# One chain of scales for the later projection weights, sums of magnitudes pinned to their place, and TensorE in program order through the opening

## The chip, the cores and the metric

The kernel runs on one core of a Trainium2 chip. The metric is the device time of one execution in microseconds (us). The engines are TensorE (PE in the profile, PEld for its weight loads), VectorE (DVE), ScalarE (ACT), GpSimd (POOL) and SyncE (SP), which issues the DMAs.

## The reference

A transformer block with parallel branches, on a sequence of 2048 rows of width 512, all in float32:

```
xn  = layernorm(x)                                    # no gain, no bias
q, k, v = xn @ wqkv                                   # 32 heads of 16
att = softmax(q k^T / 4) v                            # every row sees every row
mlp = gelu(xn @ w1 + b1) @ w2 + b2                    # 512 -> 1792 -> 512
out = x + att @ wo + mlp
```

## The kernel before, in words

**Numbers.** Matrices are multiplied as pairs of 16-bit halves: a high part and the rest, so each product of float32 operands is three matmuls. Before a weight is split into its halves it is divided by a power of two, taken from its largest magnitude (for some weights from an average of magnitudes). `scales` (L122) makes such factors: each column of a 128 x n tile holds one value per partition, TensorE transposes it (L125), VectorE takes the maximum of each row (L127), TensorE spreads the n results over all partitions (L130), and VectorE keeps the exponent bits (L137) and takes reciprocals (L139). `split_pool` (L147) then writes the halves, one instruction on ScalarE and two on GpSimd.

**Heads and units.** The query and key weights are worked off in four column blocks m = 0 to 3 of 128 columns (8 heads each). Scores are computed for groups of four heads. A *unit* is 128 queries by 512 keys of one group of four heads: `s_half` (L247) issues, for each head, four matmuls 62 x 32 (tile `pS`), and VectorE takes the row maximum of each head's scores (tile `mt`, L259), 0.6 us each. Two neighbouring heads lie on the two halves of the partitions. Scores use three PSUM banks in rotation. The maxima go through DRAM (`m_d`) into two extra rows of the queries' operand, and 19 units later (`LEAD`) the scores are computed again, transposed, with the maximum subtracted, and ScalarE takes the exponential (L304, tile `pe`). The value products (`pV`) follow. Into the gaps go matmuls of a filler: the rest of the value projection, the projections of m = 1 to 3, then the MLP and the output projection.

**The opening** is the program up to the first exponential. It loads and normalizes x in four blocks of 512 rows (`stats`, `transpose_x`), projects q and k of m = 0 for each block (`project`), stores them to `qk_d` and reads them back stacked (`stacks`, L403), computes the value projection of nine row tiles (`v_tiles`), and runs the first sixteen units, four after the projection of each block (`tile_and_unit`, L846: two heads' scores, three matmuls of the value projection, and the same again). Beside this it loads the weights w1, w2 and wo in 16 pieces of 512 KB (`chunk`, L719, three buffers, issued by SyncE), and ScalarE sums the magnitudes of each piece (`measure`, L830, instruction L835). `fetch` keeps one piece ahead. Each step of the generator `ms` is one piece; `MEASURE` says how many steps follow each unit of a block (its first entry belongs to the last four units).

**Order.** In the opening the order of each engine's instructions is chosen by a scheduler, which may move an instruction ahead of the program when it takes its operands to be ready. From unit 16 on all five engines keep the order of the program (L1022); there, `later` and `by_slots` hand out small pieces of work unit by unit.

**The later weights.** `prep_qk` (L458) takes the largest magnitudes of a pair of weight blocks (tile `wq` -> `am_qk`, L461), calls `scales` for two columns and splits. For m = 1 it is called in the opening (L927), for m = 2 and 3 in the slots, when the projection of the block before begins (L952). `prepare` (L970) makes the ten scales of w1, b1, w2 and wo in the first slots and then splits these weights.

Of the kernel before, what the change touches and what calls it, by code (L numbers as in the profile page):

```python
# [9 lines left out]
F32 = mybir.dt.float32  # L10
# [20 lines left out]
VW = DH + 1  # L31
LEAD = 19
FAST, MEAN, SLOW = (4, 4), (3, 4), (3, 3)
MEASURE = (2, 0, 1, 1)
HALF = 1300
POOL_NS = 2500
TAIL = 5
# [14 lines left out]
def layer_kernel(ctx: ExitStack, tc: tile.TileContext, x, wqkv, wo, w1, b1, w2, b2, out):  # L52
# [144 lines left out]
            product(user, dst[j:j + 32], lhs[:, j:j + 32], rhs, start=start, stop=stop)  # L197


    scale_of = {}  # L200

    def fetch_scale(m):

# [247 lines left out]
    def load_qk(m):  # L451
        wf = []
        for w in range(2):
            wf.append(ph.tile([P, D], F32, name="wq", bufs=2).rearrange("p (c n) -> p c n", n=P))
            nc.sync.dma_start(wf[w], wqkv[:, w * D + m * P:w * D + (m + 1) * P].rearrange("(c p) n -> p c n", p=P))
        return wf

    def prep_qk(m, wf, bank, ready_w):  # L458
        am = work.tile([P, 2], F32, name="am_qk", bufs=2)
# [248 lines left out]
    with ExitStack() as st1:  # L708
# [6 lines left out]
        def load_x(t):  # L715
            xs[t] = px.tile([P, D], F32, name="xs", bufs=8)
            nc.sync.dma_start(xs[t], x[t * P:(t + 1) * P, :])

        def chunk(src):  # L719
            wf = ph.tile([P, 4 * W], F32, name="wch", bufs=3)  # L720
            v = wf.rearrange("p (a b) -> p a b", b=src.shape[2])
            if len(loads) < 17:
                nc.sync.dma_start(v, src)
            else:
                later(2, lambda: nc.sync.dma_start(v, src), True)
            return v
# [9 lines left out]
        wov = wo.rearrange("(c p) n -> p c n", p=P)  # L736
        every = [w1v[:, :, i * W:(i + 1) * W] for i in range(7)]
        every = every + [w2v[:, 2 * i:2 * i + 2, :] for i in range(7)] + [wov[:, 0:2, :], wov[:, 2:4, :]]
        every = every + every
        amx = work.tile([P, 16], F32, name="amx")  # L740
        am_all = work.tile([P, 10], F32, name="am_all")
        fac1 = []

        def fetch(k):
            while len(loads) <= min(k + 1, 31):
                loads.append(chunk(every[len(loads)]))
            return loads[k]

        for t in range(4):
            load_x(t)  # L750
        wfs = [load_qk(0)]
        for t in range(4, 8):
            load_x(t)
        wvv = wqkv[:, 2 * D:3 * D].rearrange("(c p) n -> p c n", p=P)
# [41 lines left out]
        def transpose_x(sb, c):  # L796
            cs = slice(sb * QB, (sb + 1) * QB)
            pt = vbank()
            for i in range(4):
                nc.tensor.transpose(pt[:, i * P:(i + 1) * P], xs[4 * sb + i][:, c * P:(c + 1) * P], ident)  # L800
            nc.scalar.activation(xt[:, 0, c, cs], pt, AF.Copy)  # L801
            if sb and c % 2:
                pf = ph.tile([P, QB], F32, name="pf", bufs=2)
                nc.scalar.activation(pf, pt, AF.Copy)
                nc.gpsimd.tensor_tensor(xt[:, 1, c, cs], pf, xt[:, 0, c, cs], op=ALU.subtract)
            else:
                nc.vector.tensor_tensor(xt[:, 1, c, cs], pt, xt[:, 0, c, cs], op=ALU.subtract)
            if c == NC - 1:
                for t in range(4 * sb + 8, min(4 * sb + 12, NT)):
                    load_x(t)  # L810
# [19 lines left out]
        def measure():  # L830

            for n in range(16):
                v = fetch(n)
                dst = am_all[:, n:n + 1] if n < 7 else amx[:, n:n + 1]
                nc.scalar.activation(v, v, AF.Abs, scale=1.0 / SPREAD, accum_out=dst)  # L835
                yield

        ms = measure()
# [55 lines left out]
            run(whole(project(0, w, 0, ready_w[0], lambda: (vbank(), None), True)))  # L894
        for w in (1, 0):
            stacks(0, w, [0])
        free[:] = ["T", "D", "T", "V", "T"]
        for c in range(NC):
            transpose_x(1, c)
        some(pv, 2)  # L900
        for sb in range(1, NQB):
            ln = stats(sb + 1) if sb < 3 else iter(())
            for w in (1, 0):
                pj = whole(project(0, w, sb, ready_w[0], lambda: (vbank(), None)))
                for n in range(3):
                    some(pj, 4)
                    some(pv, 1)
                    if sb == 2:
                        some(ln, 3)
                run(pj)  # L910
            run(pv)
            for w in (1, 0):
                stacks(0, w, [sb])
            wfs.append(load_qk(sb))
            if sb == 1:
                clear(1)
            for j in range(4):
                tile_and_unit(4 * sb - 4 + j)
                some(ms, MEASURE[sb])
                if sb == 1:  # L920
                    some(ln, 4)
                elif sb == 2:
                    transpose_x(3, j)
            if sb == 1:
                for c in range(NC):
                    transpose_x(2, c)
        pq = prep_qk(1, wfs[1], sbank, ready_w)  # L927
        for j in range(4):
            some(pq, 2)
            tile_and_unit(NT - 4 + j)  # L930
            some(ms, MEASURE[0])
        run(pq)
        run(vs)
        nc.sync.dma_start(b1_s, b1.rearrange("(f p) -> p f", p=P))
        pos[0] = 16

# [3 lines left out]
        def rest():  # L940
            for k in range(8):
                later(8 + 4 * k, lambda k=k: stacks(1, 1 - k // 4, [k % 4]), True)
            for k in range(4 * NQB):
                c, cols = k % 4, slice(k // 4 * QB, k // 4 * QB + QB)
                later(10 + 3 * k, lambda c=c, cols=cols: nc.sync.dma_start(xn_d[:, :, c, cols], xt[:, :, c, cols]), True)
            for t in range(NV, NT):
                yield v_group(t, wvh, dbank)
            for m in range(1, 4):
                while m not in ready_w:
                    yield None  # L950
                if m < 3:
                    by_slots(prep_qk(m + 1, wfs[m + 1], sbank, ready_w))  # L952
                for sb in range(NQB):
                    for w in (1, 0):
                        yield project(m, w, sb, ready_w[m], dbank)
                    if m == 3 and sb == 2:
                        for n in range(2):
                            fetch_w1(n)
                        fetch_x(0)
# [8 lines left out]
                   (0, then))  # L968

        def prepare():  # L970
            yield from ms
            am = am_all
            nc.vector.tensor_reduce(am[:, 7:8], b1_s, axis=AX.X, op=ALU.max, apply_absolute_value=True)
            nc.vector.tensor_reduce(am[:, 8:9], amx[:, 7:14], axis=AX.X, op=ALU.max)
            nc.vector.tensor_reduce(am[:, 9:10], amx[:, 14:16], axis=AX.X, op=ALU.max)
            box = []
            yield
            yield from scales(am, 10, sbank, box)
            inv, fac = box
            fac1.append(fac)  # L980

            nc.vector.reduce_max(gs[:, 0:1], fac[:, 0:8], axis=AX.X)
            nc.gpsimd.tensor_tensor(gs[:, 3:4], fac_v[0][:, 0:1], fac[:, 9:10], op=ALU.mult)
            yield
            nc.vector.reciprocal(gs[:, 1:2], gs[:, 0:1])
            nc.gpsimd.tensor_tensor(gs[:, 2:3], gs[:, 0:1], fac[:, 8:9], op=ALU.mult)
            yield
            nc.vector.tensor_scalar_mul(gs[:, 1:2], gs[:, 1:2], 0.5)
            ended = [True]
            for n in range(16):  # L990
                v = fetch(16 + n)
                while not ended[0] or len(v_done) < NT:
                    yield
                ended[0] = False

                def then(wh=None, n=n):
                    ended[0] = True
                    later(2, lambda: put(wh, n), True)

                def put(wh, n):  # L1000
                    for a in range(2):
                        if n < 7:
                            later(a, lambda a=a: nc.sync.dma_start(w1_d[n, :, a], wh[:, a]), True)
                        elif n < 14:
                            later(a, lambda a=a: nc.sync.dma_start(w2_d[:, :, 2 * n - 14 + a], wh[:, :, a]), True)

                if n >= 14:
                    i = 2 * (n - 14)
                    split_steps(wo_s[:, 0, i:i + 2, :], wo_s[:, 1, i:i + 2, :], v, inv[:, 9:10], then)
                    continue  # L1010
                if n < 7:

                    wh = ph.tile([P, 2, 2, NC, P], F16, name="wsp", bufs=3)
                    split_steps(wh[:, :, 0], wh[:, :, 1], v.rearrange("p c (a n) -> p a c n", n=P), inv[:, n:n + 1],
                                lambda wh=wh, then=then: then(wh))
                else:
                    wh = ph.tile([P, 2, 2, D], F16, name="wsp", bufs=3)
                    split_steps(wh[:, 0], wh[:, 1], v, inv[:, 8:9], lambda wh=wh, then=then: then(wh))
            while not ended[0]:
                yield  # L1020
# [234 lines left out]
```

## Time and profile before

| | |
|---|---|
| median of 3 runs | 1506.36 us (1505.23 to 1510.21) |
| the profiled execution | 1509.12 us, span 1507.3 us |
| granted TensorE clock, mean | 0.996 |
| TensorE busy | 1484.6 us |
| VectorE busy | 1387.1 us |
| ScalarE busy | 1257.4 us |
| GpSimd busy | 661.4 us |
| first exponential | 108.5 us |
| bytes moved | 123.75 MB, mean 82 GB/s |

Times within a profile are counted from the start of the span. In a timeline row stand the start, the time from the first instruction's start to the last one's end, the engine, the line, the operation, the tiles written and read, their shapes and the number of merged instructions; in brackets the engine's idle time ahead of it and what ended that. In the chain of waits each row is the stretch by which a piece of work moved the end. SPq is SyncE issuing DMAs.

### The profile page before, as it was taken

Reading aid. Unit: us, or ns where it says so; the run is one execution under the profiler, and the core shown is the slowest. Engines: PE = TensorE matmul, PEld = TensorE weight load, DVE = VectorE, ACT = ScalarE, POOL = GpSimd, SP = SyncE. Lnnn points to the kernel's source line nnn. Section 1 sums busy time; section 2 is a strip of 40 time slices with the busy share of each in tenths; the row PEclk is TensorE's granted clock in tenths of the full one; section 3 lists DMA queues with packets and bytes.
Section 4 is the critical chain, followed back from the end, with each engine's and each line's share of the span. In section 5 each row is a group of like instructions: output and inputs, shape, how many; then the busy total and the mean of one; then the engine's idle time right before and its main releaser. Section 6 shows DMA issues by size and latency. Waiting matters only on the chain.

```text
span 1507.3 us, 87890 instructions
## 1 busy us (share of the span) xinstructions
PE 1484.6 (98%) x39995; PEld 815.2 (54%) x39995; DVE 1387.1 (92%) x2333; ACT 1257.4 (83%) x2348; POOL 661.4 (44%) x686
## 2 busy tenths in 40 slices
PE   8999999999999999999999999999999999999998
PEld 3335555555555555555555555555555555555554
DVE  8789889999899999999999999999999999999933
ACT  4738878888899888899988889998888998888884
POOL 4112778423777311377821147862115786121210
PEclk9999999999999999999999999999999999999998
DMA  8730867224222310131111111121112210211432
GB/s 248 242 95 7 247 200 238 72 73 125 85 76 73 99 29 27 42 85 43 43 57 43 51 50 39 44 78 57 37 27 61 70 36 19 57 54 33 137 92 93
DMA packets 113357, 123.75 MB, mean 82 GB/s; under 512 B 24668, under 2 KB 84956, under 8 KB 112984
## 3 DMA queue, kind: packets, MB, share of 16 engines
q1 hardware_dynamic: 112984, 118.14, 26.4%
q8 instruction: 312, 5.11, 1.4%
q14 instruction: 61, 0.50, 0.1%
HBM read 80.61 MB, written 37.34 MB: 78 GB/s over the span
## 4 chain that ended last, share of the span: by engine, by line
PE 87%; DVE 8%; issue 1%; DMA 1%; ACT 1%; POOL 0%; SPq 0%; ACTq 0%; POOLq 0%
PE pV L168 25%; PE pD L168 23%; PE pS L168 18%; PE pT L168 18%; DVE mt L259 7%; PE pT L437 1%; PE pD L437 1%; DMA wch<-in_B_w_dram 1%; PE pV L437 1%; DMA wq<-in_A_wqkv_dram 0%; DVE am_qk L461 0%; DVE mneg L270 0%; PE pT L800 0%; ACT xt L801 0%; DVE wvh L145 0%
## 5 line engine op out<-in xcount | busy, mean ns | idle before, releaser
L259 DVE TENSOR_REDUCE mt<-pS 128x1 f32<-128x512 f32 x2048 | 1308.5, 684 | 52.7 <-PE pS L168 32.5
L304 ACT ACTIVATE pe<-pT 128x512 f32<-128x512 f32 x2048 | 1111.7, 599 | 180.3 <-PE pT L168 75.0
L168 PE MATMUL pV<-pe,vv 64*32 64x512 f32 x8192 | 1075.8, 595 | 0.3 <-issue 0.2
L168 PE MATMUL pT<-qst,kst 64*32 64x512 f16 x8192 | 715.9, 377 | 3.4 <-DMA qst<-m_d 2.0
L168 PE MATMUL pS<-kst,qst 62*32 62x512 f16 x8192 | 627.9, 378 | 4.4 <-DVE mt L259 1.5
L168 PEld LDWEIGHTS <-qst 62*32 62x32 f16 x8192 | 280.8, 92 | 230.4 <-issue 62.8
L168 PEld LDWEIGHTS <-kst 64*32 64x32 f16 x8192 | 279.3, 91 | 174.9 <-issue 79.1
L168 PE MATMUL pD<-xb,wc 64*32 64x512 f16 x5376 | 360.9, 377 | 0.0
L168 PE MATMUL pD<-w_s,g 64*32 64x512 f16 x5376 | 359.4, 377 | 0.0
L168 PEld LDWEIGHTS pV<-pe,vv 64*32 64x32 f32 x8192 | 183.1, 105 | 88.5 <-PE pV L168 1.9
L168 PE MATMUL pD<-xt,wqk_h 64*32 64x512 f16 x2304 | 152.5, 378 | 1.5 <-issue 1.5
L168 PEld LDWEIGHTS <-wc 64*32 64x32 f16 x5376 | 116.6, 91 | 42.4 <-issue 0.6
L168 PEld LDWEIGHTS <-g 64*32 64x32 f16 x5376 | 112.9, 91 | 44.3 <-issue 0.4
L1097 POOL TENSOR_TENSOR xa<-xa,yt 128x512 f32<-128x512 f32 x16 | 20.4, 1276 | 237.4 <-ACT yt L1095 237.4
L360 POOL TENSOR_TENSOR osb<-osb,rb 128x512 f32<-128x512 f32 x31 | 39.8, 1284 | 192.3 <-DMA rb<-den_d 142.7
L1052 POOL TENSOR_TENSOR t<-hh 128x512 f32<-128x512 f32 x56 | 58.2, 1039 | 68.3 <-ACT hh L1072 67.6
L1047 POOL TENSOR_TENSOR t<-t,hh 128x512 f32<-128x512 f32 x56 | 71.8, 1282 | 4.7
L1054 POOL TENSOR_TENSOR t<-t,hh 128x512 f32<-128x512 f32 x56 | 71.8, 1281 | 4.7
L1049 POOL TENSOR_TENSOR g<-t,g 128x512 f16<-128x512 f32 x56 | 65.2, 1164 | 4.7
L168 PEld LDWEIGHTS <-wqk_h 64*32 64x32 f16 x2304 | 53.4, 92 | 23.2 <-issue 4.6
L1046 POOL TENSOR_SCALAR t<-t,gs 128x512 f32<-128x512 f32 x56 | 38.7, 692 | 49.8 <-ACT t L1041 49.7
L168 PE MATMUL pD<-wo_s,oc 64*32 64x512 f16 x828 | 54.5, 378 | 0.0
(147 smaller groups left out, 871.9 us busy)
## 6 DMA issues: line engine op xcount, KB each, us to landing
wch<-in_B_w_dram SPq DMA_DIRECT2D x28, 512.0 KB
wc<-w_d SPq DMA_DIRECT2D x56, 256.0 KB
qk_d<-stg SPq DMA_DIRECT2D x32, 256.0 KB
rb<-den_d SPq DMA_DIRECT2D x124, 64.0 KB
w_d<-wsp SPq DMA_DIRECT2D x28, 256.0 KB
kst<-qk_d SPq DMA_DIRECT2D x128, 48.0 KB
qst<-qk_d SPq DMA_DIRECT2D x128, 48.0 KB
xs<-in_A_x_dram SPq DMA_DIRECT2D x16, 256.0 KB
```

What stands on the lines that cost most here:

```text
L168: p = nc.tensor.matmul(*args, **kw)
L259: nc.vector.reduce_max(mt_of[t][:, n, qt, kb:kb + 1], s, axis=AX.X)
L304: nc.scalar.activation(pe, st, AF.Exp, scale=scale_of[g // 2])
L360: pooled((1280, lambda: nc.gpsimd.tensor_tensor(osb, osb, rb, op=ALU.mult)), (620, lambda: nc.gpsimd.tensor_scalar(ot[:, 0], osb, 1.0, 0.0 ...
L437: nc.tensor.matmul(self.bank, lhs, rhs, start=start, stop=self.last and self.over())
L1046: pooled((690, lambda: nc.gpsimd.tensor_scalar(t1, t1, 1.0, gs[:, 1:2], op0=ALU.add, op1=ALU.mult)), (1280, lambda: nc.gpsimd.tensor_tenso ...
L1047: (1280, lambda: nc.gpsimd.tensor_tensor(t1, t1, hh, op=ALU.mult)),
L1049: (1160, lambda: nc.gpsimd.tensor_tensor(g[:, 1, f, :], t1, g[:, 0, f, :], op=ALU.subtract)),
L1052: pooled((1040, lambda: nc.gpsimd.tensor_tensor(t1, hh, hh, op=ALU.mult)), (620, lambda: nc.gpsimd.tensor_scalar(t1, t1, 1.0, 1.0 / GELU_A ...
L1054: (1280, lambda: nc.gpsimd.tensor_tensor(t1, t1, hh, op=ALU.mult)),
L1097: add = lambda: nc.gpsimd.tensor_tensor(xa, xa, yt, op=ALU.add)
```

## The change

Three things, all in or behind the opening:

- TensorE keeps the order of the program from the second block's transposes to unit 16. The other engines' order is still the scheduler's.
- Each load of a piece and each sum of magnitudes is pinned: it may not be issued ahead of the instruction that stands before it on its engine in the program (`pin`). The steps are spread over all four groups of units (`MEASURE`).
- The weights of m = 1, 2 and 3 share the chain of scales in `prepare`, which now has 16 columns. Two more pieces of 512 KB are loaded in the opening (the q and k columns of m = 2 and 3) and VectorE takes their maxima there; those of m = 1 follow. `prep_qk` remains for m = 0 alone. `split_qk` splits a pair by a scale that is there already: for m = 1 in the first slots, for m = 2 and 3 where `prep_qk` was called. The pairs of m = 2 and 3 are loaded in the slots, after the split of the pair before.

```diff
-MEASURE = (2, 0, 1, 1)
+MEASURE = (2, 1, 1, 1)
...
+    def split_qk(m, wf, inv, ready_w):
+        wh = ph.tile([P, 2, 2, NC, P], F16, name="wqk_h", bufs=2)
+        for w in (1, 0):
+            split_pool(wh[:, w, 0], wh[:, w, 1], wf[w], inv[:, 8 + 2 * m + w:9 + 2 * m + w])
+            yield
+        ready_w[m] = wh
+        if m < 3:
+            later(4, lambda: wfs.append(load_qk(m + 1)), True)
...
+        def pin(i):
+            if loads and not pos[0]:
+                tc.keep_in_program_order(i)
+
         def chunk(src):
...
-            if len(loads) < 17:
-                nc.sync.dma_start(v, src)
+            if len(loads) <= NM:
+                pin(nc.sync.dma_start(v, src))
...
-        every = every + every
+        wqk = wqkv[:, 0:2 * D].rearrange("(c p) (w n) -> p w c n", p=P, w=2)
+        every = every + [wqk[:, w, :, W:2 * W] for w in range(2)] + every
+        NM = 18
...
-                nc.scalar.activation(v, v, AF.Abs, scale=1.0 / SPREAD, accum_out=dst)
+                pin(nc.scalar.activation(v, v, AF.Abs, scale=1.0 / SPREAD, accum_out=dst))
+                yield
+            for w in range(2):
+                v = fetch(16 + w)
+                for m in (2, 3):
+                    absmax(am_all[:, 8 + 2 * m + w:9 + 2 * m + w], v[:, :, (m - 2) * P:(m - 1) * P])
+                yield
+            for w in range(2):
+                absmax(am_all[:, 10 + w:11 + w], wfs[1][w])
                 yield
...
+        with tc.manual_schedule(engines={mybir.EngineType.PE}):
             free[:] = ["T", "D", "T", "V", "T"]
...
-            wfs.append(load_qk(sb))
+                if sb == 1:
+                    wfs.append(load_qk(1))
...
-        pq = prep_qk(1, wfs[1], sbank, ready_w)
-        for j in range(4):
-            some(pq, 2)
-            tile_and_unit(NT - 4 + j)
-            some(ms, MEASURE[0])
-        run(pq)
-        run(vs)
+                tile_and_unit(NT - 4 + j)
+                some(ms, MEASURE[0])
+            run(vs)
+            run(ms)
...
-                    by_slots(prep_qk(m + 1, wfs[m + 1], sbank, ready_w))
+                    by_slots(split_qk(m + 1, wfs[m + 1], inv1[0], ready_w))
...
         def prepare():
-            yield from ms
...
-            yield from scales(am, 10, sbank, box)
+            yield from scales(am, 16, sbank, box)
             inv, fac = box
             fac1.append(fac)
+            inv1.append(inv)
+            by_slots(split_qk(1, wfs[1], inv, ready_w))
+            nc.vector.tensor_tensor(sexp[:, 1:4], fac[:, 10:16:2], fac[:, 11:16:2], op=ALU.mult)
+            nc.vector.tensor_scalar_mul(sexp[:, 1:4], sexp[:, 1:4], DH ** -0.5)
+            yield
```

More of the change, by code (lines that the diff above doesn't have):

```diff
@@ L197, in tiled @@
             product(user, dst[j:j + 32], lhs[:, j:j + 32], rhs, start=start, stop=stop)
-    scale_of = {}
+    scale_of, wfs = {}, []
     def fetch_scale(m):
@@ L738, in layer_kernel @@
         every = every + [w2v[:, 2 * i:2 * i + 2, :] for i in range(7)] + [wov[:, 0:2, :], wov[:, 2:4, :]]
-        every = every + every
+        wqk = wqkv[:, 0:2 * D].rearrange("(c p) (w n) -> p w c n", p=P, w=2)
+        every = every + [wqk[:, w, :, W:2 * W] for w in range(2)] + every
+        NM = 18
         amx = work.tile([P, 16], F32, name="amx")
-        am_all = work.tile([P, 10], F32, name="am_all")
-        fac1 = []
+        am_all = work.tile([P, 16], F32, name="am_all")
+        fac1, inv1 = [], []
         def fetch(k):
-            while len(loads) <= min(k + 1, 31):
+            while len(loads) <= min(k + 1, NM + 15):
                 loads.append(chunk(every[len(loads)]))
@@ L750, in layer_kernel @@
             load_x(t)
-        wfs = [load_qk(0)]
+        wfs.append(load_qk(0))
         for t in range(4, 8):
@@ L896, in layer_kernel @@
             stacks(0, w, [0])
[L897 to L913, printed above, removed]
-            wfs.append(load_qk(sb))
-            if sb == 1:
-                clear(1)
-            for j in range(4):
[L918 to L926, printed above, removed]
@@ L927, in layer_kernel @@
-        pq = prep_qk(1, wfs[1], sbank, ready_w)
-        for j in range(4):
-            some(pq, 2)
-            tile_and_unit(NT - 4 + j)
-            some(ms, MEASURE[0])
-        run(pq)
-        run(vs)
+        with tc.manual_schedule(engines={mybir.EngineType.PE}):
+            free[:] = ["T", "D", "T", "V", "T"]
+            for c in range(NC):
+                transpose_x(1, c)
+            some(pv, 2)
+            for sb in range(1, NQB):
+                ln = stats(sb + 1) if sb < 3 else iter(())
+                for w in (1, 0):
+                    pj = whole(project(0, w, sb, ready_w[0], lambda: (vbank(), None)))
+                    for n in range(3):
+                        some(pj, 4)
+                        some(pv, 1)
+                        if sb == 2:
+                            some(ln, 3)
+                    run(pj)
+                run(pv)
+                for w in (1, 0):
+                    stacks(0, w, [sb])
+                if sb == 1:
+                    wfs.append(load_qk(1))
+                if sb == 1:
+                    clear(1)
+                for j in range(4):
+                    tile_and_unit(4 * sb - 4 + j)
+                    some(ms, MEASURE[sb])
+                    if sb == 1:
+                        some(ln, 4)
+                    elif sb == 2:
+                        transpose_x(3, j)
+                if sb == 1:
+                    for c in range(NC):
+                        transpose_x(2, c)
+            for j in range(4):
+                tile_and_unit(NT - 4 + j)
+                some(ms, MEASURE[0])
+            run(vs)
+            run(ms)
@@ L990, in prepare @@
             for n in range(16):
-                v = fetch(16 + n)
+                v = fetch(NM + n)
                 while not ended[0] or len(v_done) < NT:
```

## The prediction

> **What bounds the kernel now.** I read the page first (shares, then the chain that ended last), then busy time by windows, then the timelines of TensorE, VectorE and SyncE up to the first exponential, and last the chain in the slots that prepare the later weights.
>
> ```profile
> span 1507.3 us, 87890 instructions
> PE 1484.6 (98%) x39995; PEld 815.2 (54%) x39995; DVE 1387.1 (92%) x2333; ACT 1257.4 (83%) x2348; POOL 661.4 (44%) x686
> PE 87%; DVE 8%; issue 1%; DMA 1%; ACT 1%; POOL 0%; SPq 0%; ACTq 0%; POOLq 0%
> 33.70:94.50 60.80, 59.65 (x430) 21.57 (x429) 50.46 (x100) 34.82 (x65) 11.77 (x11) 1.00 0.64 194
> 94.50:107.20 12.70, 12.70 (x112) 4.78 (x114) 8.66 (x20) 2.37 (x4) 0.00 (x0) 1.00 0.33 96
> 140.00:240.00 100.00, 96.60 (x2688) 52.77 (x2672) 90.78 (x159) 79.89 (x151) 70.00 (x61) 1.00 0.67 208
> 107.24 1.28 ACT L304 ACT_TABLE_LOAD   x1
> ```
>
> TensorE is the bound and VectorE is close behind it. In the window rows the columns are window, length, then PE, PEld, DVE, ACT and POOL busy, clock, DMA share and GB/s. The change touches two stretches. One is the opening: of the 60.8 us in which the sixteen early units run, TensorE is busy for 59.65 and VectorE for 50.46. The other is 140 to 240 us, where the scales of weights 2 and 3 are made. From 107 us on nothing else is moved, so a gain or a loss ahead of the first exponential passes to the end of the kernel in full.
>
> A busy TensorE need not be an efficient one:
>
> ```profile
> 34.58 0.40 PE L168 MATMUL pS<-kst,qst 62*32 62x512 f16 x4
> 34.91 0.60 PE L437 MATMUL pV<-wvh,xt 128*128 128x512 f16 x2
> 35.45 0.40 PE L168 MATMUL pS<-kst,qst 62*32 62x512 f16 x4
> 52.46 0.41 PE L168 MATMUL pS<-kst,qst 62*32 62x512 f16 x8
> 52.80 0.82 PE L437 MATMUL pD<-wvh,xt 128*128 128x512 f16 x3
> 53.55 0.50 PE L168 MATMUL pS<-kst,qst 62*32 62x512 f16 x8
> 93.12 0.40 PE L168 MATMUL pS<-kst,qst 62*32 62x512 f16 x4
> 71.31 11.10 DVE L259 TENSOR_REDUCE mt<-pS 128x1 f32<-128x512 f32 x18 [1.55 <-PE pS L168]
> ```
>
> A half unit is two groups of four score matmuls, on the two halves of the rows. Issued together they take 8 matmuls and 3 of the value projection from 52.46 to 53.55: 1.09 us. Issued apart, 4 scores and 2 of the value projection take 34.58 to 35.45: 0.87 us. A value matmul is (0.82-0.39)/2, about 0.215 us, by the ends of a group of three and of one; so four scores apart cost 0.44 us, and eight together 1.09-0.65=0.44 us as well. A pair that is split costs 0.44 us more. Between 33 us and the last one above I count 38 groups of four that stand apart, so 19 pairs: 8.3 us. In the program the two halves follow each other at once.
>
> **The change part by part.** *TensorE in program order.* Its work in the opening stretch falls by those 8.3 us to about 51.4. But VectorE has 50.46 us of work there, and in the clean part above one maximum takes 11.10/18=0.617 us, so a half unit takes 1.23 us on VectorE against 1.09 on TensorE. VectorE becomes the bound of the early units. I therefore take the gain by pieces. The first eight units I put at 0 to 1.3 us: VectorE limits them already. The last eight run from 70.86 to the first maximum of unit 16:
>
> ```profile
> 70.86 0.41 PE L168 MATMUL pS<-kst,qst 62*32 62x512 f16 x8
> 95.95 1.29 DVE L259 TENSOR_REDUCE mt<-pS 128x1 f32<-128x512 f32 x2 [1.43 <-PE pS L168]
> 145.66 0.60 DVE am_qk L461
> 148.65 0.59 DVE am_qk L461
> ```
>
> They take 25.1 us now. Afterwards VectorE has 32 x 0.617=19.7 us of maxima, and four more maxima of weight pieces (128x512, 0.60 each by the rows of the same form): 2.4 us, so 22.1. TensorE has 16 x 1.09 and 12 x 0.215, 20.0 us. The gain is 3.0 us if the data is there. The two maxima of weight 1 already ran early and may again; if they come at the end they cost 1.2 us.
>
> *Sums in the program's place.* Now ScalarE takes them as soon as its order allows, ahead of work that matters:
>
> ```profile
> 21.53 1.06 ACT L835 ACTIVATE wch<-wch 128x1024 f32<-128x1024 f32 x1 [1.27 <-DMA wch<-in_B_w_dram]
> 22.59 1.32 ACT L785 ACTIVATE xs<-xs,sd 128x512 f32<-128x512 f32 x2
> 48.89 3.95 DMA wch<-in_B_w_dram
> 54.20 0.16 DVE L773 TENSOR_TENSOR sd<-sd 128x4 f32<-128x4 f32 x1 [0.60 <-ACT sd L769]
> 57.62 0.37 SPq L494 DMA_DIRECT2D qk_d<-stg  x1
> 60.70 1.70 SPq L403 DMA_DIRECT2D qst<-qk_d  x4
> 62.50 5.86 SPq L723 DMA_DIRECT2D wch<-in_B_w_dram  x4
> 78.70 0.41 SPq L723 DMA_DIRECT2D wch<-in_B_w_dram  x1
> ```
>
> The first sum (1.06 us) stands ahead of the rows that the transposes at 22.8 us wait for; behind them it gives back 0 to 1.1 us, and I take 0.7. The second place is a load of 3.95 us on the chain, behind which the square root of the third row block came late (VectorE idle 0.60 for it): 0 to 1.3 us, I take 0.8, and this is the same gain as that of the first eight units, counted once.
>
> What it costs is the queue. From the sixth piece on a load is issued behind the stacks of its block, and those behind the projections' stores. Now the loads were free to go first, and the last was issued at 78.70. From store to load it takes 62.50-57.62=4.9 us. If the projection of the last block ends near 69.4 and its store goes out at 71.8, the pieces 9 to 17 start at 76.2. Three buffers turn in a load of about 4 us (3.95 above) and a sum of 1.25 (1.06 and the read of its total), so three pieces per 5.3 us: nine are there at 76.2+15.8=92, and the maxima of the last end at 93 to 94, against 92.3 by VectorE's work alone. TensorE has value matmuls to do meanwhile. I take off 1.5 us, between 0 and the whole 3.0 of the case below. Two pieces of 512 KB come new, and one pair of weight loads of 256 KB each leaves the opening; at the 194 GB/s of the stretch the net 0.5 MB is 2.7 us of transfer, inside the train just told.
>
> Behind a late piece wait VectorE's maxima of the scores, and behind those TensorE, which has three banks for scores; on ScalarE the evictions of the value projection wait behind a late sum; on SyncE the row maxima of unit 16.
>
> *One chain of scales.* The scales of weights 2 and 3 leave the slots:
>
> ```profile
> 217.41 0.59 DVE am_qk L461
> 220.40 0.59 DVE am_qk L461
> 151.15 0.21 PE pS L125
> 151.36 0.33 PE pS L168 x4
> 151.70 0.38 PE pS L168 x4
> 154.28 0.31 PE pS L130 x2
> 154.59 0.33 PE pS L168 x4
> 89.16 1.34 ACT L148 ACTIVATE wqk_h<-wq,inv 128x512 f16<-128x512 f32 x2 [2.02 <-DVE inv L139]
> ```
>
> All of these but the last stand on the chain. Each preparation gives back 1.19 us of maxima, 0.52 us of small TensorE work, and up to 0.5 us because the bank that it takes splits a pair (0.33+0.38 against 0.44, twice). VectorE's end is followed closely by TensorE's, busy for 96.6 of 100 us, so I take 1.19+0.5 each, 3.4 for two (0 if TensorE fills the place at once, at most 4.4). The split of weight 1 (1.34 us of ScalarE, and its GpSimd part) moves from the opening into the first slots, where ScalarE is free for about a fifth of the time by the last window row; 0 to 1.3, I take 0.4. The chain of scales itself is 16 columns in place of 10 with the same instructions, and two small products for three weights replace two for each; nothing.
>
> **The sum.** 0.7+0.8+3.0-1.5+3.4-0.4 is 6.0 us less. The profiled execution took 1509.12 us (span 1507.3 and 1.8 around it), 2.8 above the median of the runs, so 1503.1 on its own scale; on the median, 1506.36-6.0=1500.4.
>
> **The rivals.** *All of TensorE's surplus comes back.* If VectorE does not become the bound because its work fits between the projections, the 8.3 us count in place of 3.0+0.8, and no load waits: 0.7+8.3+3.0=12.0, 1494.4. Against it stands VectorE's 50.46 of 60.8 us with work to be added.
>
> *The loads eat the opening.* If the train of nine pieces ends 3 us later than told, the opening gives nothing and the slots' 3.0 stay (3.4-0.4): 1503.4. For it speaks that SyncE's queue already held up ScalarE.
>
> *Slower: the train turns slowly.* In the timelines VectorE, ScalarE and SyncE each work off their instructions in one order, so a late load holds what stands behind it. If each turn of three pieces takes 8.7 us in place of 5.3, because a sum waits behind evictions and the next load behind that sum, the last piece lands at 76.2+26.1=102.3, its maxima end near 103.5 and unit 16 starts 7.5 us after 95.95. Less the slots' 3.0 and the 0.7, and with 1.0 for a second block whose loads hold the transposed rows up, that is 4.8 us more, 1511.2. The opening loses from the point where a turn takes over 6.2 us (the maxima then end at 96), the kernel as a whole from about 7.1. The 4.80 us that the first load takes make it possible:
>
> ```profile
> 16.71 4.80 DMA wch<-in_B_w_dram
> 20.00:22.00 2.00, 0.88 (x4) 0.18 (x2) 2.00 (x8) 0.73 (x2) 0.00 (x0) 1.00 0.82 150
> 22.00:24.00 2.00, 0.93 (x7) 0.66 (x7) 2.00 (x6) 2.00 (x5) 0.00 (x0) 1.00 0.63 136
> 24.00:26.00 2.00, 2.00 (x10) 2.00 (x11) 1.43 (x3) 1.91 (x4) 0.00 (x0) 0.51 0.85 273
> 26.00:28.00 2.00, 2.00 (x9) 0.91 (x8) 0.70 (x3) 2.00 (x5) 1.44 (x2) 0.64 0.92 250
> ```
>
> *The clock falls.* Here TensorE was busy for 1.81 of 4 us, and in the 4 us that follow the granted clock was 0.51 and 0.64: 0.98+0.72=1.7 us lost. In program order TensorE has nothing beside the transposes ahead of the second and third block's projections; should it idle like this at both, 3.4 us go and the time is 1503.8. Against it: those waits are an eviction long, about 1 to 2 us, not 4. The Trainium skill, "TensorE: Matmul & The Clock Gate", Part 1, has the clock fall to half after an idle window of about 3.4 us. By that rule waits of 1 to 2 us cost nothing; the rows above show it falling after a stretch that was only half idle, so I keep a chance for it.
>
> *The change does not do what it says:* the half units stay apart since the second group waits for a bank. Then VectorE is what it waits for, and that is the forecast's own case.
>
> **How the numbers follow.** The forecast has 0.45 (1497 to 1503.5 by its own bounds), all of the surplus 0.20, the eaten opening 0.15, slower 0.15, the clock 0.05. A measurement of this kernel tells about 0.3% (4.5 us) from no change, that is 1501.8 and 1510.9. Of the forecast two thirds (0.30) lie below 1501.8 with the whole second case: faster 0.5 and a little for a mix of the two, 0.53. Same: 0.15 of the forecast, 0.15, 0.05, less that little: 0.32. Slower 0.15. The range 1494 to 1508 leaves out most of the slower case and little else.
>
> **What would show it.** Right: nearly all score matmuls of the opening in groups of eight; VectorE's idle time there down to a few us; the first exponential's table load at 104 to 105 in place of 107.24, the rest of the gain between 140 and 240; no VectorE maxima of weights in the slots. The eaten opening and the slow train show as VectorE waiting for a load near 90 us with SyncE's last loads past 88. Wrong: a table load later than 107.24, or a clock under 0.9 between 40 and 95 us.

## The result: slower by 0.65%, and the profile after

The changed kernel takes 1519.43 us (median of 7 runs, 1514.68 to 1524.13), the kernel before beside it 1509.76 us (7 runs, 1505.23 to 1512.71). The ratio is 1.0065, 95% interval 1.0047 to 1.0083: slower by about 9.7 us, where 6.0 us less was forecast. The prediction was wrong. The late pieces of its rival "the train turns slowly" did come, but mainly since the train started late, and the work ahead of it was late as well.

The page and the windows of the changed kernel:

```profile
span 1513.8 us, 87872 instructions
PE 1476.7 (98%) x39986; PEld 818.1 (54%) x39986; DVE 1384.8 (91%) x2317; ACT 1257.5 (83%) x2348; POOL 661.8 (44%) x686
PE 82%; DVE 9%; DMA 3%; issue 2%; SPq 1%; ACT 1%; POOL 1%; DVEq 0%; ACTq 0%; POOLq 0%
```

```profile
33.70:94.50 60.80, 52.78 (x410) 20.77 (x408) 45.89 (x84) 32.25 (x61) 8.47 (x7) 0.94 0.56 172
94.50:107.20 12.70, 8.12 (x60) 2.93 (x53) 7.68 (x16) 4.87 (x9) 0.00 (x0) 0.85 0.64 201
140.00:240.00 100.00, 96.69 (x2755) 54.27 (x2740) 89.38 (x145) 81.29 (x154) 69.13 (x59) 1.00 0.58 182
```

TensorE is busy for 8 us less than before in the whole kernel, and the span is 6.5 us longer. On the chain that ended last the DMA's share went from 1% to 3%. In the opening both engines stand idle for longer: TensorE from 59.65 to 52.78 busy us, VectorE from 50.46 to 45.89, with a clock of 0.94. In the 12.7 us after that, where TensorE was always busy before, it works for 8.12 at a clock of 0.85. In the slots TensorE does as much as before in the same 100 us, and VectorE 1.4 us less: the maxima of the weights are gone from there.

VectorE's timeline of the changed kernel, from the maxima of the last eight early units to the first negated row maxima (`mneg`) and the first maximum of unit 16, and ScalarE's, in which the table load marks the first exponential:

```profile
77.99 19.22 DVE L259 TENSOR_REDUCE mt<-pS 128x1 f32<-128x512 f32 x32 [1.55 <-PE pS L168]
101.38 1.28 DVE L742 TENSOR_REDUCE am_all<-wch 128x1 f32<-128x512 f32 x2 [4.16 <-DMA wch<-in_A_wqkv_dram]
103.48 1.28 DVE L742 TENSOR_REDUCE am_all<-wch 128x1 f32<-128x512 f32 x2 [0.83 <-DMA wch<-in_A_wqkv_dram]
104.68 0.21 DVE L270 TENSOR_REDUCE mneg<-mt 128x16 f32<-128x64 f32 x1
104.80 1.28 DVE L259 TENSOR_REDUCE mt<-pS 128x1 f32<-128x512 f32 x2
```

```profile
45.54 1.06 ACT L850 ACTIVATE wch<-wch 128x1024 f32<-128x1024 f32 x1 [5.65 <-DMA wch<-in_B_w_dram]
87.91 1.06 ACT L850 ACTIVATE wch<-wch 128x1024 f32<-128x1024 f32 x1 [4.99 <-DMA wch<-in_B_w_dram]
117.99 1.28 ACT L304 ACT_TABLE_LOAD   x1
```

The same instructions on VectorE in the kernel before; one later `mneg` of each kernel follows, from behind the slots that prepare the weights:

```profile
94.30 0.22 DVE L270 TENSOR_REDUCE mneg<-mt 128x16 f32<-128x64 f32 x1
142.48 0.22 DVE L270 TENSOR_REDUCE mneg<-mt 128x16 f32<-128x64 f32 x1
799.60 0.22 DVE L270 TENSOR_REDUCE mneg<-mt 128x16 f32<-128x64 f32 x1
```

```profile
153.22 0.22 DVE L270 TENSOR_REDUCE mneg<-mt 128x16 f32<-128x64 f32 x1
807.86 0.22 DVE L270 TENSOR_REDUCE mneg<-mt 128x16 f32<-128x64 f32 x1
```

I use `mneg` as a marker. The first one comes 10.38 us later than before (104.68 against 94.30), the table load 10.75 later, the second `mneg` 10.74, the one near 800 us 8.26. So the loss is made ahead of the first exponential, and about 2.5 us of it come back between the second marker and the one near 800 us. The 10.38 us add up from three pieces of VectorE's time:

- The maxima of the last eight units start at 77.99 instead of 71.31: 6.68 later.
- They take 19.22 us instead of 22.99 (71.31 to 94.30): 3.77 less. The program's order does what was forecast.
- Behind them VectorE waits for the last two pieces and takes their maxima, from 97.21 to 104.68: 7.47 more.

The first piece is TensorE's. Its timeline in the changed kernel:

```profile
47.71 0.38 PE L437 MATMUL pT<-xt,wqk_h 128*128 128x512 f16 x1 [1.93 <-ACT xt L816]
...
50.95 6.82 PE L437 MATMUL pT<-xt,wqk_h 128*128 128x512 f16 x20 [1.14 <-POOL xt L820]
57.70 0.41 PE L168 MATMUL pS<-kst,qst 62*32 62x512 f16 x8
...
74.43 0.59 PE L437 MATMUL pT<-xt,wqk_h 128*128 128x512 f16 x2 [2.38 <-POOL xt L820]
77.55 0.41 PE L168 MATMUL pS<-kst,qst 62*32 62x512 f16 x8
...
105.03 0.43 PE L277 MATMUL pS<-ident,mneg 64*32 64x64 f32 x4 [4.51 <-DVE mneg L270]
```

Scores go in groups of eight, as the change says. But ahead of the third block's projection TensorE waits, and in the projection itself the clock falls (granted 0.66 from 51 to 58 us). ScalarE's first row above shows why it waits longer than an eviction: the pinned sum at 45.54 sat at the head of ScalarE's queue for 5.65 us, until its load came, and the copies of the transposed rows stood behind it. The last block's projection waits again, and its scores start at 77.55 instead of 70.86.

The third piece is the load train. SyncE's timeline of the changed kernel:

```profile
80.06 0.36 SPq L503 DMA_DIRECT2D qk_d<-stg  x1
82.19 1.70 SPq L403 DMA_DIRECT2D qst<-qk_d  x4
83.94 7.03 SPq L736 DMA_DIRECT2D wch<-in_B_w_dram  x5
91.94 2.92 SPq L736 DMA_DIRECT2D wch<-in_A_wo_dram  x2
96.82 1.65 SPq L736 DMA_DIRECT2D wch<-in_A_wqkv_dram  x2
```

Nine pieces stand behind the last stacks. The stores go out late since the projection was late, so the train starts at 83.94. VectorE's two maxima rows then show when the last two landed: at 101.4 and 103.5. TensorE stands still behind them for 4.51 us (its last row above), and its clock falls a second time.

### The profile page after: what moved, and what is told of

It reads as the page before. It is cut to its first block, busy times and chain, and to the rows that moved or that the text cites. A ratio compares the mean times of both kernels' runs of the same rounds, so it can differ in the third digit from the quotient of the medians.

```text
span 1513.8 us, 87872 instructions
## 1 busy us (share of the span) xinstructions
PE 1476.7 (98%) x39986; PEld 818.1 (54%) x39986; DVE 1384.8 (91%) x2317; ACT 1257.5 (83%) x2348; POOL 661.8 (44%) x686
## 4 chain that ended last, share of the span: by engine, by line
PE 82%; DVE 9%; DMA 3%; issue 2%; SPq 1%; ACT 1%; POOL 1%; DVEq 0%; ACTq 0%; POOLq 0%
PE pV L168 24%; PE pD L168 22%; PE pT L168 17%; PE pS L168 17%; DVE mt L259 7%; PE pT L437 1%; DMA qk_d<-stg 1%; DMA wch<-in_B_w_dram 1%; DMA m_d<-mhl 1%; PE pD L437 1%; DMA wch<-in_A_wqkv_dram 0%; DMA wch<-in_A_wo_dram 0%; DMA xs<-in_A_x_dram 0%; ACT wch L850 0%; SPq L367 0%
## 5 line engine op out<-in xcount | busy, mean ns | idle before, releaser
L1079 POOL TENSOR_TENSOR t<-hh 128x512 f32<-128x512 f32 x56 | 58.2, 1040 | 69.4 <-ACT hh L1099 68.6
```

Source lines behind the costliest of these rows:

```text
L1079: pooled((1040, lambda: nc.gpsimd.tensor_tensor(t1, hh, hh, op=ALU.mult)), (620, lambda: nc.gpsimd.tensor_scalar(t1, t1, 1.0, 1.0 / GELU_A ...
```

## The experiments

In each, the kernel named first is the changed one unless the text says "before". Times are medians beside runs of the kernel before on the same chip, ratios are to that kernel, with 95% intervals. A profile is one execution: those of e5 to e8 and of e11 lie 3.2 to 5.3 us below the median of their kernel, so rows show where time goes and the ratios say what it is worth.

**Which of the three parts costs.** Four kernels take the parts alone or in pairs.

e1_no_pins: the loads and sums may move again; the chain and TensorE's order stay.

```diff
-                pin(nc.sync.dma_start(v, src))
+                nc.sync.dma_start(v, src)
...
-                pin(nc.scalar.activation(v, v, AF.Abs, scale=1.0 / SPREAD, accum_out=dst))
+                nc.scalar.activation(v, v, AF.Abs, scale=1.0 / SPREAD, accum_out=dst)
```

> The changed kernel with no pins: neither the loads of the pieces nor the sums are held in their place; TensorE's order and the one chain stay. Theory A (the pinned loads stand behind the stacks, so the pieces come late: VectorE waits for the last two at 97 to 103 us, TensorE idles and its clock falls): the table load of the first exponential comes at 104 to 108 us in place of 117.99, the total is 4 to 8 us below the kernel before. Theory B (TensorE's own order costs: ahead of the second and third block's projections it waits for evictions, which the scheduler's order had filled): the waits near 46 to 51 and 71 to 74 us stay, the table load is at 110 to 113, the total within 3 us of the kernel before.

Measured: 1506.37 us, 0.9990 (0.9974 to 1.0007). The loss is gone. VectorE's timeline of this kernel:

```profile
71.09 16.83 DVE L259 TENSOR_REDUCE mt<-pS 128x1 f32<-128x512 f32 x28 [1.51 <-PE pS L168]
87.84 2.45 DVE L742 TENSOR_REDUCE am_all<-wch 128x1 f32<-128x512 f32 x4
90.22 2.47 DVE L259 TENSOR_REDUCE mt<-pS 128x1 f32<-128x512 f32 x4
92.72 0.22 DVE L270 TENSOR_REDUCE mneg<-mt 128x16 f32<-128x64 f32 x1
```

No wait for a piece, and the first `mneg` 1.58 us earlier than before. TensorE's third projection keeps its clock: its twenty matmuls take 4.64 us.

```profile
47.41 0.38 PE L437 MATMUL pT<-xt,wqk_h 128*128 128x512 f16 x1 [0.69 <-ACT xt L816]
49.13 4.64 PE L437 MATMUL pT<-xt,wqk_h 128*128 128x512 f16 x20 [1.34 <-POOL xt L820]
```

e11_pins_no_order: pins and chain stay, TensorE's order is the scheduler's again.

```diff
-        with tc.manual_schedule(engines={mybir.EngineType.PE}):
+        if True:
```

> The changed kernel without TensorE's program order, pins and one chain kept. If the pins and the maxima of the last pieces are the cause by themselves: VectorE still waits for the last pieces, first row maxima at 100 to 105, total 5 to 10 us above the kernel before. If they cost only together with TensorE's order, since it made the second and third block late: first row maxima at 95 to 98, total within 3.

Measured: 1509.14 us, 1.0011 (0.9994 to 1.0028). VectorE's timeline:

```profile
71.31 11.10 DVE L259 TENSOR_REDUCE mt<-pS 128x1 f32<-128x512 f32 x18 [0.86 <-PE pS L168]
...
95.39 1.28 DVE L742 TENSOR_REDUCE am_all<-wch 128x1 f32<-128x512 f32 x2 [1.95 <-DMA wch<-in_A_wqkv_dram]
96.59 0.21 DVE L270 TENSOR_REDUCE mneg<-mt 128x16 f32<-128x64 f32 x1
```

With the same pins the last eight units start where they did before, the train starts at 77.98, and the wait for the pieces is 1.95 us. The first `mneg` is 2.29 us later than before; by the marker near 800 us the kernel is 1.74 ahead (797.86). The pins by themselves don't make the loss.

e3_chain_only: both edits together, so that only the chain and the two pieces are left.

> The changed kernel with neither pins nor TensorE's order: only the one chain of scales with its two pieces more in the opening. If the slots give back what the two traces say (6.5 us of span lost at the end against 10.75 at the first exponential, so 4.3 gained after it) and the two pieces cost nothing: table load at 107 to 108, total 4 us below the kernel before. If the two pieces cost their transfer (2.7 us) or their wait: table load at 109 to 111, total 1 to 3 below or even.

Measured: 1507.49 us, 0.9998 (0.9980 to 1.0015). Its first `mneg` is 3.45 us later than before, since the scheduler puts the maxima of the pieces (2.46 us at 91.71) between those of the scores; by the marker near 800 us it stands 1.45 later.

e4_pe_only: the kernel before, with TensorE's order alone.

```diff
+        with tc.manual_schedule(engines={mybir.EngineType.PE}):
```

> The kernel before with TensorE in program order through the opening and nothing else. Theory A: the split pairs go and nothing is waited for that was not before; table load at 102 to 105 in place of 107.24, total 2 to 5 us below the kernel before. Theory B: TensorE waits for evictions ahead of the two projections, table load at 109 to 112, total 2 to 5 us above.

Measured: 1509.45 us, 1.0006 (0.9989 to 1.0024); first `mneg` 1.79 us later than before. The order alone brings nothing.

What follows from the four: with the chain as the base (0.9998), adding the order gives 0.9990 and adding the pins 1.0011. If the two added up, all three would give 1.0003. The changed kernel is at 1.0065. So about 0.6%, 9.4 us, belongs to the pair: neither part has it alone. Four intervals of about 0.17% each make 0.35% on this difference, so the difference is clear of zero. With the chain, neither makes the last block late alone: the last eight units start at 71.09 with the order and no pins (e1), at 71.31 with the pins and no order (e11), and at 77.99 with both. In its order TensorE has no other work while a pinned sum on ScalarE holds up the copies that a projection needs; the pinned loads then stand behind the late block.

**Which of the pins.** e2_loads_free takes the pin from the loads alone, e5_sums_free from the sums alone (one line of e1's diff each).

> The changed kernel with the pins on the loads alone taken away; sums stay pinned. Theory A: the loads are what matters, so nearly all comes back, table load at 106 to 110, total 2 to 6 us below the kernel before. Rival A2 (the pinned sums hold the buffers, so the loads cannot run ahead however free they are): the last pieces are still awaited near 95 us or later, table load at 112 to 117, total 2 to 6 us above the kernel before.

> The changed kernel with the pins on the sums alone taken away; the loads stay pinned behind the stacks. If the loads' pin is what makes the pieces late: the last two pieces are still awaited past 95 us, first row maxima (the instruction that closes unit 15) at 102 to 105 against 94.30 before and 104.68 changed, total 5 to 9 us above the kernel before. If the sums' place counts as much: first row maxima at 96 to 100, total 1 to 4 above.

Measured: e2 1510.34 us, 1.0015 (0.9994 to 1.0036); e5 1514.93 us, 1.0045 (1.0028 to 1.0062). VectorE's timeline of e5:

```profile
73.15 19.23 DVE L259 TENSOR_REDUCE mt<-pS 128x1 f32<-128x512 f32 x32 [1.55 <-PE pS L168]
95.81 1.28 DVE L742 TENSOR_REDUCE am_all<-wch 128x1 f32<-128x512 f32 x2 [3.44 <-DMA wch<-in_A_wqkv_dram]
98.10 1.28 DVE L742 TENSOR_REDUCE am_all<-wch 128x1 f32<-128x512 f32 x2 [1.01 <-DMA wch<-in_A_wqkv_dram]
99.30 0.21 DVE L270 TENSOR_REDUCE mneg<-mt 128x16 f32<-128x64 f32 x1
```

With the sums free the last eight units start 4.84 us earlier than in the changed kernel (73.15 against 77.99), and the twenty matmuls of the third projection run at full clock (4.65 us). The train is as it was: 6.9 us from the end of the maxima to `mneg`, against 7.47. With the loads free it is the other way round: ScalarE still waits 5.59 us at the head of its queue, TensorE's twenty matmuls are slow (6.16 us), the last eight start at 75.04, and the waits for the pieces shrink to 1.00 and 0.33 us. The pinned loads make the late pieces, the pinned sums the late projections, and of the two the loads cost more, by a difference (0.30%) just outside its noise.

**Is it VectorE behind the late pieces?** e6_mid keeps everything, pins included, and moves the two new pieces up: eighth and ninth to be loaded, and their maxima before the last block in place of at the end of the train. The other nine stay behind the stacks.

```diff
-        every = every + [wqk[:, w, :, W:2 * W] for w in range(2)] + every
+        every = every[:7] + [wqk[:, w, :, W:2 * W] for w in range(2)] + every[7:] + every
...
-                v = fetch(n)
+                v = fetch(n if n < 7 else n + 2)
...
+                if n == 6:
...
-                v = fetch(16 + w)
+                        v = fetch(7 + w)
```

> The changed kernel, all pins kept, with the two query and key pieces loaded after the seventh piece in place of last, their maxima behind unit 7. The pieces come as late as before, but no VectorE maximum stands behind the last ones; only sums on ScalarE do. If what costs is VectorE waiting at 97 to 103 us and the clock after it: first row maxima 6 to 8 us earlier than in the changed kernel (97 to 99), total 6 to 8 us below it, so 1 to 4 above the kernel before. If late pieces cost by another way (the row maxima's store behind them on SyncE, or the buffers): less than 3 us come back.

Measured: 1507.06 us, 0.9999 (0.9985 to 1.0012). Its train is still late: SyncE issues loads of pieces from 79.28 to 93.24. Timelines of VectorE and ScalarE:

```profile
73.27 19.23 DVE L259 TENSOR_REDUCE mt<-pS 128x1 f32<-128x512 f32 x32 [1.00 <-PE pS L168]
92.53 0.22 DVE L270 TENSOR_REDUCE mneg<-mt 128x16 f32<-128x64 f32 x1
```

```profile
96.34 1.06 ACT L850 ACTIVATE wch<-wch 128x1024 f32<-128x1024 f32 x1 [0.55 <-DMA wch<-in_A_wo_dram]
```

The last sum ends after `mneg` and nobody waits for it. The first `mneg` comes 12.15 us earlier than in the changed kernel, where 6 to 8 were expected: 7.47 because no maximum of a piece stands ahead of it, the rest because the last eight units start 4.72 earlier (in this profile the clock held). So a late train cost nothing by itself here; it costs what stands behind it on an engine that the scores need.

**What the clock is worth.** e7_warm adds 14 matmuls, whose result nothing uses, between the third block's transposes and its projection.

```diff
+                    wp = banks("S")
+                    for _ in range(14):
+                        nc.tensor.matmul(wp, wvh[0][:, 0, 0:P], wvh[0][:, 0, :], start=True, stop=True)
```

> The changed kernel with 14 matmuls on data already there, their result unused, behind the transposes of the third row block (about 3 us of TensorE work into a gap that is 3.6 us idle in all). If the half clock between 51 and 57 us is what stretches the 20 matmuls there from about 4.6 to 6.82 us: they take 4.5 to 4.8, and the first row maxima come 1.5 to 2.5 us earlier if nothing else waits. If the pieces' train sets the end anyway (its next load goes out behind the stacks of this block): the train moves by the same 1.5 to 2.5 us. Total about 2 below the changed kernel.

Measured: 1517.44 us, 1.0061 (1.0041 to 1.0081). TensorE's and VectorE's timelines:

```profile
50.22 4.66 PE L437 MATMUL pT<-xt,wqk_h 128*128 128x512 f16 x20 [0.58 <-POOL xt L820]
71.70 4.44 PE L437 MATMUL pV<-xt,wqk_h 128*128 128x512 f16 x12
```

```profile
76.52 19.23 DVE L259 TENSOR_REDUCE mt<-pS 128x1 f32<-128x512 f32 x32 [2.98 <-PE pS L168]
100.55 2.67 DVE L742 TENSOR_REDUCE am_all<-wch 128x1 f32<-128x512 f32 x4 [4.81 <-DMA wch<-in_A_wqkv_dram]
103.14 0.21 DVE L270 TENSOR_REDUCE mneg<-mt 128x16 f32<-128x64 f32 x1
```

At the third projection the clock was restored (4.66 us against 6.82), but it fell at the last one, behind a wait of 2.38 us: its last twelve matmuls take 4.44 us, where the changed kernel needs 2.75. So the added matmuls moved the fall, and what a full clock through both projections is worth stays open. The last eight units came 1.5 us earlier, and so did the first `mneg`; VectorE waits 4.81 us for the pieces there. The time does not tell this kernel from the changed one.

**A version that beats both.** e8_nopins_mid joins e6's order of the pieces with e1's free loads and sums. e9_mid_no_order is e8 without TensorE's order, and e10_mid_again is e8 once more, timed beside e9.

> No pins, and the two query and key pieces after the seventh: their maxima fall into the third block's projection, where VectorE waited for 2.4 and 1.5 us in the run without pins, and not in front of unit 15's maxima, where TensorE then waited for 2.09. First row maxima 1.5 to 2.5 us earlier than without pins (90 to 91.5), total 1.5 to 2.5 us below that kernel, about 3 to 4 below the kernel before. If the two gaps are not on the path: no change from the run without pins.

> The best kernel so far (no pins, the two pieces after the seventh) without TensorE's program order. If the order is worth the 3.0 us that the forecast gave it for the last eight units: first row maxima about 3 us later than with it (94 to 95 against 91.26), total 2 to 4 us above that kernel. If VectorE is the bound either way: within 1 us.

> No pins and the two pieces after the seventh, once more beside the kernel without TensorE's order: ratio to the kernel before 0.996 to 0.999, as in the first series (0.9976).

Measured: e8 1503.98 us, 0.9976 (0.9959 to 0.9993); e9 1505.09, 0.9972 (0.9956 to 0.9988); e10 1503.24, 0.9972 (0.9952 to 0.9992). VectorE of e8, then of e9:

```profile
67.25 1.86 DVE L742 TENSOR_REDUCE am_all<-wch 128x1 f32<-128x512 f32 x3
...
72.00 19.22 DVE L259 TENSOR_REDUCE mt<-pS 128x1 f32<-128x512 f32 x32 [0.88 <-PE pS L168]
91.26 0.22 DVE L270 TENSOR_REDUCE mneg<-mt 128x16 f32<-128x64 f32 x1
```

```profile
93.19 0.22 DVE L270 TENSOR_REDUCE mneg<-mt 128x16 f32<-128x64 f32 x1
```

The maxima of the pieces now lie in front of the last block's projection, where VectorE waits for TensorE anyway. That is about 0.25% faster than before. TensorE's order brings the first `mneg` 1.5 to 1.9 us earlier (e10, e8 against e9), which the times don't tell from nothing. The order alone (e4) and the chain alone (e3) bring nothing; the gain is in the chain with its maxima early.

## Why the prediction was wrong, point by point

**Two terms of the sum failed, and the larger is the start of the last eight units.** The forecast's own measure is the first maximum of unit 16: at 95.95 before, it was to come 3.0 us earlier. It came at 104.80, 8.85 later. Of the 11.9 us between the two, 8.2 are the start of the last eight units, 3.5 the wait for the pieces and 0.2 the stretch itself.

**The load train** was put at 1.5 us lost, and VectorE waited 4.99 (4.16 and 0.83). A start at 76.2 was taken, and 5.3 us for each turn of three pieces. The train started at 83.94 and its last piece landed about 103.5, so nine pieces took 19.5 us, 6.5 a turn. Of the 11.5 us by which the last piece was later than the forecast 92, 7.7 are the start and 3.7 the turns (19.5 against 15.8). The way from the store to the load was about right (3.9 us here from the last store; the forecast's row gave 4.9 and its sum used 4.4), but the projection was taken to end near 69.4, and it ended at 77.6. In e11, where the last block was on time, the train starts at 77.98 and VectorE waits 1.95 us. That is no test of the 1.5: VectorE ended the maxima of the scores there at 93.44, 2.9 us later than 19.22 us from 71.31 would give.

**The projections were the step in front of it.** The sum gave 0.7 for the first sum and 0.8 for the third block, so the last eight units should have started 1.5 us earlier; they started 6.7 later. The third block's projection waited 3.6 us in all and the last one 3.2, and the clock took 2.2. I had seen that in program order TensorE has nothing beside the projections, and put it away in the rival of the clock at 1.7 us each. Two things were missed. A pinned sum waits for its load at the head of ScalarE's queue (5.65 us) and the copies that feed the projection stand behind it: the prediction named this for the value projection's evictions, not for these. And from a late projection everything pinned behind it is late, which made the two rivals one.

**The last eight units themselves went as told.** Without the waits for pieces, the stretch from their first scores to the first maximum of unit 16 is 22.3 us (77.55 to 104.80, less 4.99); 22.1 were forecast, 25.1 it was before. VectorE became the bound: its maxima run 19.22 us without a gap. But this is a gain in one stretch, and in TensorE's order a wait ahead of it reaches TensorE at once. In e4, which has the order alone, a sum that nobody pinned waits 2.83 us for its piece at 65.67, ahead of the copies, and the clock falls to 0.50 (70 to 72 us); the maxima start at 74.77, 3.46 us later than before.

**The slots** can't be judged so finely. 3.4 us were forecast, less 0.4 for the split of weight 1. From the first to the second `mneg` 0.36 us are lost, but e4, whose split stays in the opening, loses 1.10 there, so the split isn't shown to be the reason. From the second to the one near 800 us 2.48 come back. The eleven profiles with the chain give back from -0.1 (e3) to 6.1 us (e6) between these markers, 2.4 in the middle; e8 and e10, one kernel twice, 3.25 and 0.35; e4, without the chain, 0.2. The forecast lies inside this scatter.

**The slower rival** had the place and the sign: a late piece, VectorE's maxima behind it, SyncE's last loads past 88, a table load past 107.24. Its mechanism, the slow turn, is the smaller part of the lateness. Its turn of 8.7 us was too long and its start too early, so it is luck that its time for the last piece nearly agrees (102.3 forecast, 103.5 measured). It put the kernel 4.8 us above the one before; the medians say 9.7 (with more runs the one before moved from 1506.36 to 1509.76 itself). The rest is the last eight units, which it let start on time, the clock, and 3.2 us by which the medians differ more than the two profiled executions (6.47), which no trace here can show. Its chance of 0.15 looks low in hindsight: the load of 4.80 us spoke for it, and against it stood one load of 3.95 us.

**The clock** fell at the third block's projection, for 2.2 us (6.82 against 4.65), and again after TensorE's wait of 4.51 us for the first `mneg` (in this row of the changed kernel 0.50 is the clock; it was 1.00 before):

```profile
104.00:108.00 4.00, 2.89 (x16) 0.90 (x16) 3.82 (x12) 0.00 (x0) 0.00 (x0) 0.50 0.02 4
```

What the second fall costs is not seen by itself: from the first `mneg` to the table load the changed kernel takes 13.31 us, and e1, whose clock held, 13.64. By the Trainium skill, "TensorE: Matmul & The Clock Gate", Part 1, the clock falls after an idle window of about 3.4 us. The second fall agrees with that; ahead of the first no single gap was longer than 1.93 us, so the rule as I had read it would have said no fall. The same section calls the window free-running; the runs below fit that better than the length of a gap.

**Left open:** whether pins would cost on TensorE's order without the chain was not tried. Why the runs scatter by 9 us is open too. Between the last two markers of the changed kernel the distance to before falls from 8.2 to 6.2 us; it falls by 0.15 to 2.0 in every other profile, e4's among them, so this is not the work of the change.

## What to carry to other kernels

Look at order constraints on two engines together: pins cost nothing measurable while the scheduler could give TensorE other work during a wait (e11), and TensorE's order cost nothing while no pinned sum stood ahead of the copies that it needed (e1); both at once cost 0.6%. Before a load is put behind a store that reads back, ask which in-order engine consumes it, and what of the critical path stands behind that consumer; if it is moved to a point where the engine idles anyway, a late train can cost nothing (e6). Sum the lateness of a stage from its first instruction on, and let each rival's delay start the next one.

## What the runs showed of the hardware

I had not expected the clock to fall on gaps this short, or to depend on so little. For the third projection, waits of 1.93, 0.35, 0.21 and 1.14 us were followed by 6.82 us for twenty matmuls, and 1.12, 0.35, 0.20 and 1.34 (e6) by 4.65; 0.69 and 1.34 (e1) by 4.64, and 1.35 and 1.34 by 6.16 (e10, below). e8, the same kernel as e10, shows 0.38 and 1.34 and then 4.64. At the last projection of e7, 0.59 and 2.38 were followed by 4.44 us for twelve matmuls that take 2.75 in the changed kernel, there after 0.85 and 2.38. So waits of one size can take a third off the speed of what follows or leave it alone, and the next profile of the same kernel may come out the other way. TensorE's timeline of e10:

```profile
47.46 0.38 PE L437 MATMUL pT<-xt,wqk_h 128*128 128x512 f16 x1 [1.35 <-ACT xt L816]
49.18 6.16 PE L437 MATMUL pT<-xt,wqk_h 128*128 128x512 f16 x20 [1.34 <-POOL xt L820]
```

A second one is the read back of the row maxima. In e3 it held TensorE up for 3.69 us at 247 us, the granted clock was 0.50 from 246 to 252 us, and that kernel loses 4.9 us between the markers at 239 and 284 us (TensorE's timeline of e3):

```profile
247.47 0.65 PE L168 MATMUL pT<-qst,kst 64*32 64x512 f16 x8 [3.69 <-DMA qst<-m_d]
```
